# Weight-sum stores recut and moved to ScalarE's DMA queue, with the first group's token loads in halves

## The chip, the cores and the metric

The kernel runs on one core of a Trainium2 chip. Its metric is device time in microseconds. Before the change the median of three runs is 1089.1 us (1088.97 to 1090.56). The profiles are of one execution each.

TensorE (PE) multiplies, VectorE (DVE) and GpSimd (POOL) do elementwise work, ScalarE (ACT) does activations and copies. A DMA is issued by an engine's instruction queue, here by SyncE (SP, which does nothing else) or by ScalarE, and then runs beside the engines. An issue stands in its engine's program order: what comes behind it waits until it has been issued.

## The reference

Linear attention with exponential features over 8 batches and 8 heads (576 tokens of 64 elements), then a feed-forward layer over all 4608 tokens of 512 elements:

```python
proj = q_or_k @ w_phi                      # 64 -> 128
proj -= max(abs(proj), axis=-1)
phi  = concat(exp(proj), exp(-proj))       # 256 features
kv, z = phi(k).T @ v, sum(phi(k))
x    = (phi(q) @ kv) / (phi(q) @ z + 1e-6) # heads side by side: 4608 x 512
h    = x @ w_in                            # 512 -> 2048
out  = (h - tanh(h)) @ w_out               # 2048 -> 512
```

The two feed-forward weights arrive as 64-bit floats and are decoded on the chip.

## The kernel before

The program is written in the order in which each engine executes it; no planner moves anything. It has two stages.

**Attention.** 32 units (a batch and a pair of heads each) go through a software pipeline. After a ramp for units 0 to 2 the loop runs `period(i)` for i = 3 to 31, then `drain()`. In period i, unit a = i is projected, c = i-1 gets its key-value product, p = i-2 its numerator, r = i-3 its denominator, q = i-4 has its reciprocal denominators spread over partitions, and o = i-5 is finished. The steps that matter here, by engine queue and in order:

- SyncE: `x_store(o)` (L495, xs<-d, 288 KB), `den_recip_load(r)` (L474, dn), `den_spread(q)` (L489, rb<-rr, two transfers of 144 KB), `load_v(a)` (L306, v, 320 KB), `den_store(r)` (L484, rr<-rn), and then at the end of the period `x0_load` (L529, in periods 17 to 20) and the stores of `aside_at(i, 2)` (`ring_store`, L112, wd<-wr).
- ScalarE: copies for the weights (`aside_at(i, False)`), the DMA of a piece of weight (L266 or L271, rawi or rawo, 512 KB), the DMA of unit i+2's q and k (L302, qk, 576 KB, which waits until the projection has read the buffer's old contents), then `denom_copy` (L469, dd), `ksum_copy` (L419, kst), the decoder's first step (L278), exponentials, `kv_copy`, `num_copy(p)` (L465, d<-po) and the last exponential.
- GpSimd: `den_mul(o)` (L492, d<-d,rb, which needs rb), `kadd(c)`, and the sums of weights.
- TensorE: project pj, pa, pt (L326), denominators and key sums (pu, L455 and L413), transposes, `kv` (L392), `num` (L441). The projection pa writes the PSUM bank that `num_copy` of the period before reads, and `num_copy` writes one of three buffers d, which `x_store` must have read: in period i it is the buffer that `x_store(i-5)` empties.

**Weight sums.** The feed-forward layer multiplies 2 x 2 blocks with seven products instead of eight. For that, sums and differences of weight blocks are formed once, split into a high and a low part (`Prep`, tiles wr, in three parts for each of eight blocks k: 512, 512 and 768 KB) and stored to DRAM (wd). Seven of the eight blocks are made during the attention periods, in steps that hang on a table `aside`: entry i holds what period i adds on ScalarE, on GpSimd and, third, as stores. Block n (in order) begins at period o = 5, 8, 12, 15, 19, 22, 26.

**Tokens.** The feed-forward layer takes its tokens from xs in groups of 768. Those of group 0 are loaded while attention still runs, as four blocks of 384 KB, each two chunks of 128 features by 384 tokens (`x0_load`). The sums that use them run in periods 30 and 31 and in the drain.

**Feed-forward.** `head()`, `frame(q)` and `finish()`: 48 steps, all after the attention stage. They load the stored weight sums again (L976).

Of the kernel before, what the change touches and what calls it, by code (L numbers as in the profile page):

```python
# [28 lines left out]
def f32(ap):  # L29
    return ap.bitcast(F32)  # L30
# [3 lines left out]
def tile_linear_attention_moe(  # L34
# [10 lines left out]
    nc = tc.nc  # L45
# [14 lines left out]
    HT = TG // 2  # L60
# [27 lines left out]
    xs = [dram.tile([NHP, P, PC], F32, name=f"xs{i}") for i in range(NBP)]  # L88
# [3 lines left out]
    wi, wo, ring, xop = {}, {}, {}, {}  # L92
    xop_pool, st_pool, xst = {s: xo for s in XO_FIRST}, [stp], {}
# [14 lines left out]
    def flat(t):  # L108
        return f32(t).rearrange("p a n f -> p (a n f)")

    def ring_store(q, n, a=0, b=None, queue=nc.sync):
        queue.dma_start(wd[q % NFP][n][:, a:b], flat(ring[q][n])[:, a:b])  # L112
# [96 lines left out]
    def st_any(n, shape, nm):  # L209
        pool = st_pool[n == 2]  # L210
        return pool.tile(shape, F32, tag=f"st{n}", name=nm)

    def st_tile(g, n, nm):
        xst[g, nm] = st_any(n, [P, 2, HT], f"xst{g}{nm}")
        return xst[g, nm]
# [11 lines left out]
    with ExitStack() as c1:  # L227
# [71 lines left out]
        def load(u, queue=nc.sync):  # L299
            u.qk = pq.tile([P, PC], F32, tag="qk", name=f"qk{u.i}")  # L300
            for o, w in ((0, PC),) if u.i else ((5 * P, PC), (0, 5 * P)):
                queue.dma_start(u.qk[:, o:w], qkT[u.i][:, o:w])  # L302
# [6 lines left out]
        def project(u, parts):  # L309
            for part in parts:  # L310
                if u.t is None:
                    u.t = [pq.tile([P, 2, 5, F], F32, tag="t0", name=f"t{u.i}_0"), None]
                    u.m = [p2.tile([P, 2, 5], F32, tag="m0", name=f"m{u.i}_0"), p2.tile([P, 2, 4], F32, tag="m1", name=f"m{u.i}_1")]
                if part == "j":
                    u.pj = ps_pj.tile([P, 2, 512], F32, tag="pj", name=f"pj{u.i}")
                    bank, tiles = u.pj, range(4)
                elif part == "t":
                    u.pt = ps_t.tile([P, 2, 512], F32, tag="pt", name=f"pt{u.i}")
                    bank, tiles = u.pt, range(4, 5)
                else:  # L320
                    u.pa = ps_d.tile([P, 2, 512], F32, tag="po", name=f"pa{u.i}")
                    bank, tiles = u.pa, range(5, 9)
                for k, a in enumerate(tiles):
                    for e in range(2):
                        hs = slice(e * D, (e + 1) * D)
                        nc.tensor.matmul(  # L326
                            bank[:, e, k * F : (k + 1) * F], u.qk[hs, a * P : (a + 1) * P], wph[hs, :], start=True, stop=True
                        )
# [10 lines left out]
        def centre(u, parts, h=None):  # L339
            for part in parts:  # L340
                x, m, t = part_of(u, part)
                if h is not None:
                    x, m, t = x[:, :, h], m[:, :, h], t[:, :, h]
                nc.vector.tensor_reduce(m, x, AX.X, ALU.max, apply_absolute_value=True)
                nc.vector.tensor_tensor(t, x, m.unsqueeze(3).broadcast_to(list(t.shape)), ALU.subtract)  # L345
# [54 lines left out]
        def kadd(u):  # L400
            x = p2.tile([P, 2, 2, F], F32, tag="ss", name=f"ss{u.i}")
            nc.gpsimd.tensor_tensor(x, u.kp[:, :, 1], u.kp[:, :, 2], ALU.add)
            nc.gpsimd.tensor_tensor(x, x, u.kp[:, :, 3], ALU.add)
            nc.gpsimd.tensor_tensor(x, x, u.kp[:, :, 4], ALU.add)
            nc.gpsimd.tensor_tensor(x, x, u.kp[:, :, 0], ALU.add)
            u.ss = x
# [60 lines left out]
        def denom_copy(u):  # L467
            u.dd = pd.tile([P, CH], F32, tag="dd", name=f"dd{u.i}")
            nc.scalar.activation(u.dd, u.pd, AF.Identity, bias=bias_t[:, 3:4])  # L469
# [21 lines left out]
        def den_mul(u, pin=lambda ins: ins):  # L491
            pin(nc.gpsimd.tensor_tensor(u.d, u.d, u.rb, ALU.mult))  # L492

        def x_store(u):
            nc.sync.dma_start(xs[u.b // 2][u.hp, :, (u.b % 2) * S : (u.b % 2 + 1) * S], u.d)  # L495
# [17 lines left out]
        def unit(i):  # L513
            return units[i] if 0 <= i < NU else None

        def bank():
            return ps_c.tile([P, 512], F32, tag="pu", name="pu")
# [5 lines left out]
                    nc.tensor.transpose(u.pq[e][:, j * P : (j + 1) * P], u.t[0][:, e, j, :], ident)  # L523
            q_turn_rest(u, u.pt[:, 0])

        def x0_load(n):
            m, c, h = ((0, 0, 0), (4, 0, 1), (6, 1, 1), (1, 1, 0))[n]
            dst = st_tile(0, 1, "b12") if m == 4 else f32(xop[0][m][:, 1])
            nc.sync.dma_start(dst, xs[0][2 * c : 2 * c + 2, :, h * HT : (h + 1) * HT].rearrange("c p t -> p c t"))  # L529

        def x0_sum(n, eng=nc.gpsimd):
            x = xop[0]
            b11, b21, b22 = (f32(x[m][:, 1]) for m in (0, 1, 6))
            b12 = xst[0, "b12"]
            if n == 0:
                eng.tensor_tensor(st_tile(0, 3, "t1"), b12, b11, ALU.subtract)
            if n == 1:
                eng.tensor_tensor(b12, b22, b12, ALU.subtract)
            if n == 2:
                eng.tensor_tensor(st_tile(0, 4, "t2"), b22, xst[0, "t1"], ALU.subtract)  # L540
            if n == 3:
                eng.tensor_tensor(st_tile(0, 0, "b21"), b21, xst[0, "t2"], ALU.subtract)
# [12 lines left out]
        aside = collections.defaultdict(lambda: ([], [], []))  # L555
        for n, k in enumerate(order[:EARLY_K]):
            p = Prep(k, nc.gpsimd, early_tile, early_stage).steps()
            o = 5 + 7 * (n // 2) + 3 * (n % 2)
            acts = ((1, "h2"), (2, "h4 h6"), (3, "h0")) if n % 2 == 0 else ((2, "h2 h6"), (3, "h4 h0"))
            work = (  # L560
                ((0, "s1 s3 s2"), (1, "s4 l2"), (2, "l4 l6"), (3, "l0"))
                if n % 2 == 0
                else ((0, "s1"), (1, "s3 s2 s4"), (2, "l2 l6"), (3, "l4 l0"))
            )
            for which, x in enumerate((acts, work)):
                for d, names in x:
                    aside[o + d][which].extend(p[nm] for nm in names.split())
            if True:
                when = (3, 4, 5, 5) if n % 2 else (2, 3, 4, 5)
                for d, (part, a, b) in zip(when, ((1, 0, 1024), (2, 0, 768), (2, 768, 1536), (0, 0, 1024))):  # L570
                    aside[o + d][2].append(lambda k=k, part=part, a=a, b=b: ring_store(k, part, a, b))
        aside[30][1].extend(lambda n=n: x0_sum(n) for n in range(2))
        aside[31][1].append(lambda: x0_sum(2))

        def aside_at(i, late):
            for f in aside[i][late]:
                f()
# [57 lines left out]
        def period(i):  # L635
            a, c, p, r, q, o = (unit(i - n) for n in range(6))
            w = dec[i - 3]
            if i < NU - 1:
                aside_at(i, False)
            if o:  # L640
                den_mul(o)
                x_store(o)
            project(a, "jat")
            centre(a, "jt")
            kadd(c)
            aside_at(i, True)
            dec.append(dec_load(i - 2, nc.scalar))
            if i + 2 < NU:
                load(units[i + 2], nc.scalar)
            pu = bank()  # L650
            if r:
                denom(r, pu)
            ksum(p, pu)
            if r:
                denom_copy(r)
                den_recip_load(r)
            if q:
                den_spread(q)
            if i > 3:
                load_v(a)  # L660
            ksum_copy(p)
            kv_turn(p)
            kv_turn_copy(p)
            dec_0(w, a.pt)
            q_turn(c)
            ksum_turn(p)
            q_turn_rest(c, pu)
            q_exp(c)
            q_exp_rest(c)
            ksum_turn_copy(p)  # L670
            centre(a, "a")
            k_exp(a, 0)
            kv(c)
            kv_copy(c)
            k_exp(a, 1, (0,))
            dec_1(w)
            dec_2(w)
            if r:
                den_recip(r)
                den_store(r)  # L680
            dec_3(w)
            if i == NU - 1:
                x0_split(0)
            if 17 <= i < 21:
                x0_load(i - 17)
            aside_at(i, 2)
            num(p)
            num_copy(p)
            if i < NU - 1:
                k_exp(a, 1, (1,))  # L690
# [610 lines left out]
```

## Time and profile before

| | |
|---|---|
| median of the runs | 1089.1 us (1088.97 to 1090.56) |
| profiled execution, its own time | 1092.86 us |
| its span | 1090.8 us |
| granted TensorE clock, mean | 0.997 |
| attention periods 3 to 31 begin | 23.68 us to 299.66 us |

Instructions are named by line, engine, operation and tile: "L326 PE MATMUL pj<-wph,qk" writes pj from wph and qk. An engine's name with a q (ACTq, SPq) is its instruction queue, where DMA issues stand; their duration is that of the issue, not of the transfer. In the chain of waits "DMA xs<-d" is a transfer from its issue to its landing. "[1.88 <-PE pu L413]" is the engine's idle time just before, and what ended it. In a table of windows each row is a stretch of the span: its length, then busy time of each engine with the count of instructions, then the granted clock of TensorE as a share of full speed, the mean busy share of the 16 DMA engines and what they moved in GB/s.

### The profile page before, as it was taken

The page shows a single profiled execution, that of the slowest core. Times are in us where ns is not written, and L with a number is a line of the kernel's source. Part 1 is how long each engine was busy: PE and PEld are TensorE (multiplying, and loading weights), DVE is VectorE, ACT ScalarE, POOL GpSimd, SP SyncE. Part 2 cuts the span into 40 slices and gives each one's busy share as a digit, 9 for nine tenths or more (in the row PEclk, how much of TensorE's full clock was granted, in tenths as well). Part 3 has the DMA queues.
Part 4 walks back from the last instruction along what each step waited for, and adds up shares of the span by engine and source line. Part 5 has one row for each costly group of instructions (what it writes and reads, how often), then busy time and mean ns, then how long its engine had stood idle before and what let it go on. Part 6 is the DMA issues. An engine that isn't in the chain of part 4 may idle for free.

```text
span 1090.8 us, 19205 instructions
## 1 busy us (share of the span) xinstructions
PE 1066.3 (98%) x7244; PEld 891.1 (82%) x7244; DVE 958.8 (88%) x1207; ACT 861.6 (79%) x1349; POOL 273.5 (25%) x236
## 2 busy tenths in 40 slices
PE   8999999899999999999999999999999999999998
PEld 6666666567657888889899889989899989989997
DVE  7999898799888999988998889988998889988877
ACT  5888887688788878887788878887778878887775
POOL 4788987789890000000000000000000000000000
PEclk9999999999999999999999999999999999999999
DMA  5689888979855363355434533355333543453311
GB/s 179 183 244 271 267 267 255 294 215 282 263 171 165 109 224 131 116 176 196 131 107 160 202 116 107 124 186 174 107 124 127 180 158 117 134 173 108 117 49 58
DMA packets 75100, 184.59 MB, mean 169 GB/s; under 512 B 15616, under 2 KB 30336, under 8 KB 75008
## 3 DMA queue, kind: packets, MB, share of 16 engines
q1 hardware_dynamic: 60608, 150.99, 42.6%
q10 hardware_dynamic: 14400, 32.38, 9.4%
q8 instruction: 57, 0.93, 0.4%
q14 instruction: 35, 0.29, 0.1%
HBM read 149.49 MB, written 33.70 MB: 168 GB/s over the span
## 4 chain that ended last, share of the span: by engine, by line
PE 78%; DVE 7%; DMA 7%; ACT 3%; issue 2%; POOL 1%; SPq 1%; ACTq 0%; DVEq 0%; POOLq 0%
PE A L142 16%; PE B L142 12%; PE po L936 11%; PE po L935 11%; PE po L941 10%; DMA xs<-d 4%; PE pc L392 4%; PE po L441 3%; PE pu L455 3%; PE pa L326 2%; DMA rb<-rr 2%; PE pj L326 2%; PE ptt L356 2%; POOL d L492 1%; DVE s2y L895 1%
## 5 line engine op out<-in xcount | busy, mean ns | idle before, releaser
L142 PE MATMUL A<-xo,wr 128*128 128x384 f32 x1152 | 233.8, 338 | 2.3 <-ACT u L855 2.2
L142 PEld LDWEIGHTS A<-xo,wr 128*128 128x128 f32 x1152 | 205.3, 188 | 16.3 <-ACT u L855 3.4
L142 PE MATMUL B<-xo,wr 128*128 128x384 f32 x864 | 176.9, 340 | 4.5 <-DVE hx L862 2.5
L142 PEld LDWEIGHTS B<-xo,wr 128*128 128x128 f32 x864 | 153.7, 189 | 11.9 <-DVE hx L862 6.0
L855 ACT COPY u<-A 128x384 f32<-128x384 f32 x144 | 69.0, 480 | 92.6 <-PE A L142 92.1
L935 PE MATMUL po<-who,ghy 128*128 128x512 f32 x288 | 113.0, 392 | 1.1 <-ACT ghy L910 1.1
L935 PE MATMUL po<-who,ghx 128*128 128x512 f32 x288 | 113.4, 394 | 0.2 <-DVE hy L866 0.2
L936 PE MATMUL po<-wlo,ghx 128*128 128x512 f32 x288 | 113.2, 393 | 0.0
L936 PE MATMUL po<-wlo,ghy 128*128 128x512 f32 x288 | 112.9, 392 | 0.0
L492 POOL TENSOR_TENSOR d<-d,rb 128x576 f32<-128x576 f32 x32 | 45.5, 1423 | 217.9 <-DMA rb<-rr 206.9
L381 ACT ACTIVATE kp<-t 64x256 f32<-64x256 f32 (+1 forms) x126 | 88.5, 727 | 2.1 <-DVE t L345 1.0
L941 PE MATMUL po<-who,glx 128*128 128x512 f32 x288 | 81.5, 391 | 0.0
L941 PE MATMUL po<-who,gly 128*128 128x512 f32 x282 | 79.8, 391 | 0.0
L392 PE MATMUL pc<-kp,v 128*64 128x256 f32 x640 | 76.1, 384 | 0.5 <-DVE kv L434 0.5
L910 ACT CAST ghy<-s2y 128x768 fp32r<-128x768 f32 x47 | 39.3, 837 | 43.9 <-DVE s2y L904 43.9
L892 DVE SCALAR_TENSOR_TENSOR s1x<-s1x,yx 128x768 f32<-128x768 f32 (+1 forms) x49 | 46.2, 942 | 27.6 <-ACT s1x L880 27.2
L441 PE MATMUL po<-qe,kv 128*64 128x288 f32 x512 | 68.0, 408 | 0.0
L941 PEld LDWEIGHTS po<-who,glx 128*128 128x128 f32 x288 | 54.0, 188 | 12.0
L392 PEld LDWEIGHTS pc<-kp,v 128*64 128x64 f32 x640 | 43.0, 136 | 24.4 <-issue 4.5
L941 PEld LDWEIGHTS po<-who,gly 128*128 128x128 f32 x282 | 52.9, 188 | 11.8
L935 PEld LDWEIGHTS po<-who,ghy 128*128 128x128 f32 x288 | 54.0, 188 | 9.7 <-ACT ghy L910 1.4
L935 PEld LDWEIGHTS po<-who,ghx 128*128 128x128 f32 x288 | 54.3, 189 | 9.1 <-DVE hy L866 0.7
(179 smaller groups left out, 2441.4 us busy)
## 6 DMA issues: line engine op xcount, KB each, us to landing
wr<-wd SPq DMA_DIRECT2D x92, 512.0 KB
wr<-wd SPq DMA_DIRECT2D x46, 768.0 KB
qk<-in_qkT ACTq DMA_DIRECT2D x27, 576.0 KB
v<-in_v SPq DMA_DIRECT2D x32, 320.0 KB
rb<-rr SPq DMA_DIRECT2D x64, 144.0 KB
xs<-d SPq DMA_DIRECT2D x32, 288.0 KB
out<-o SPq DMA_DIRECT2D x35, 256.0 KB
rawo<-in_moe_w_out ACTq DMA_DIRECT2D x16, 512.0 KB
```

The lines of the kernel that those rows point to most:

```text
L142: nc.tensor.matmul(bank[:, 0:HT], w[:, a, n, cs], x[:, b, c, :], start=start and i == 0, stop=i == 5, skip_group_check=not start,)
L326: nc.tensor.matmul(bank[:, e, k * F : (k + 1) * F], u.qk[hs, a * P : (a + 1) * P], wph[hs, :], start=True, stop=True)
L381: nc.scalar.activation(u.kp[h, :, j, s, :], u.t[r][h, :, x, :], AF.Exp, scale=1.0 - 2.0 * s)
L392: nc.tensor.matmul(u.pc[e * D : (e + 1) * D, 0 : 2 * F], u.v[:, j, e, :], u.kp[:, e, j, :, :], start=(j == first), stop=(j == last))
L441: nc.tensor.matmul(u.po[e * D : (e + 1) * D, c, 0:CH], u.kv[:, s, e * D : (e + 1) * D], u.qe[:, e, s, c * CH : (c + 1) * CH], start=(s == ...
L492: pin(nc.gpsimd.tensor_tensor(u.d, u.d, u.rb, ALU.mult))
L855: nc.scalar.copy(t, A[q][:, 0:HT])
L892: nc.vector.scalar_tensor_tensor(z.s1[:, s], z.s1[:, s], PC1, z.y[:, s], ALU.add, ALU.mult)
L910: nc.scalar.copy(z.gh[:, s], z.s2[:, s])
L935: nc.tensor.matmul(po, z.gh[:, ts], wh, start=first, stop=False)
L936: nc.tensor.matmul(po, z.gh[:, ts], wl, start=False, stop=False)
L941: nc.tensor.matmul(po, z.gl[:, ts], wh, start=False, stop=last)
```

## The change

The stores of a block's sums are cut anew, so that each of the periods 8 to 31 stores 512 KB (period 7: 256 KB). Before it was 384, 512 or 896 KB. There are 35 stores instead of 28. Each of the four token loads becomes two of 192 KB, one for each chunk, in consecutive periods: periods 9 and 10, 11 and 12, 16 and 17, 18 and 19, instead of 17 to 20. Both kinds are issued by ScalarE instead of SyncE. Their place in the period moves: from its end to just behind the DMA of unit i+2's q and k, ahead of the denominators. In periods 8 to 22 and 27 to 29 ScalarE issues two of them, in the others of 7 to 31 one.

```diff
-        def x0_load(n):
+        def x0_load(n, j):
             m, c, h = ((0, 0, 0), (4, 0, 1), (6, 1, 1), (1, 1, 0))[n]
-            dst = st_tile(0, 1, "b12") if m == 4 else f32(xop[0][m][:, 1])
-            nc.sync.dma_start(dst, xs[0][2 * c : 2 * c + 2, :, h * HT : (h + 1) * HT].rearrange("c p t -> p c t"))
+            if m == 4 and j == 0:
+                st_tile(0, 1, "b12")
+            dst = xst[0, "b12"] if m == 4 else f32(xop[0][m][:, 1])
+            nc.scalar.dma_start(dst[:, j], xs[0][2 * c + j, :, h * HT : (h + 1) * HT])
...
-            if True:
-                when = (3, 4, 5, 5) if n % 2 else (2, 3, 4, 5)
-                for d, (part, a, b) in zip(when, ((1, 0, 1024), (2, 0, 768), (2, 768, 1536), (0, 0, 1024))):
-                    aside[o + d][2].append(lambda k=k, part=part, a=a, b=b: ring_store(k, part, a, b))
+            pieces = (
+                ((2, 1, 0, 512), (3, 1, 512, 1024), (3, 2, 0, 512), (4, 2, 512, 1536), (5, 0, 0, 1024))
+                if n % 2 == 0
+                else ((3, 1, 0, 1024), (4, 2, 0, 1024), (5, 2, 1024, 1536), (5, 0, 0, 512), (6, 0, 512, 1024))
+            )
+            for d, part, a, b in pieces:
+                aside[o + d][2].append(lambda k=k, part=part, a=a, b=b: ring_store(k, part, a, b, nc.scalar))
+        for i, m in ((9, 0), (11, 3), (16, 1), (18, 2)):
+            for c in range(2):
+                aside[i + c][2].append(lambda m=m, c=c: x0_load(m, c))
...
             if i + 2 < NU:
                 load(units[i + 2], nc.scalar)
+            aside_at(i, 2)
             pu = bank()
...
-            if 17 <= i < 21:
-                x0_load(i - 17)
-            aside_at(i, 2)
             num(p)
```

## The prediction

> **What bounds the kernel now.** I read the page first: busy shares and the chain that ended last.
>
> ```profile
> span 1090.8 us, 19205 instructions
> PE 1066.3 (98%) x7244; PEld 891.1 (82%) x7244; DVE 958.8 (88%) x1207; ACT 861.6 (79%) x1349; POOL 273.5 (25%) x236
> PE 78%; DVE 7%; DMA 7%; ACT 3%; issue 2%; POOL 1%; SPq 1%; ACTq 0%; DVEq 0%; POOLq 0%
> qk<-in_qkT ACTq DMA_DIRECT2D x27, 576.0 KB
> v<-in_v SPq DMA_DIRECT2D x32, 320.0 KB
> rb<-rr SPq DMA_DIRECT2D x64, 144.0 KB
> xs<-d SPq DMA_DIRECT2D x32, 288.0 KB
> rawo<-in_moe_w_out ACTq DMA_DIRECT2D x16, 512.0 KB
> ```
>
> TensorE is the bound, yet 7% of the chain is DMA. Only the attention periods move in this change. The timeline of TensorE gives their starts (the pj projections of L326): period 3 at 23.68, period 8 at 71.46, period 31 at 299.66. A table of windows, each from one such start to the next, shows periods 9, 13, 14, 18 to 22, 27 and 29.
>
> ```profile
> 23.68 1.06 PE L326 MATMUL pj<-wph,qk 64*128 64x128 f32 x16
> 71.46 1.16 PE L326 MATMUL pj<-wph,qk 64*128 64x128 f32 x16
> 299.66 1.16 PE L326 MATMUL pj<-wph,qk 64*128 64x128 f32 x16
> core 0: us, PE busy (x) PEld busy (x) DVE busy (x) ACT busy (x) POOL busy (x), PEclk, DMA share, GB/s
> 80.88:90.30 9.42, 9.42 (x111) 6.54 (x109) 8.61 (x14) 7.29 (x15) 8.42 (x8) 1.00 0.88 245
> 118.57:128.57 10.00, 9.75 (x111) 6.64 (x109) 8.71 (x14) 8.15 (x16) 8.79 (x8) 1.00 0.88 263
> 128.57:138.00 9.43, 9.43 (x112) 6.55 (x110) 8.55 (x12) 7.96 (x17) 8.79 (x8) 1.00 0.89 284
> 166.26:175.69 9.43, 9.43 (x111) 6.56 (x110) 8.55 (x12) 8.33 (x17) 9.06 (x8) 1.00 0.81 251
> 175.69:186.87 11.18, 9.82 (x111) 6.63 (x109) 8.57 (x12) 7.39 (x15) 8.00 (x8) 1.00 0.82 255
> 186.87:197.44 10.57, 9.64 (x112) 6.64 (x110) 8.57 (x12) 7.91 (x16) 8.49 (x9) 1.00 0.88 272
> 197.44:209.07 11.63, 9.62 (x112) 6.74 (x110) 8.77 (x12) 8.34 (x17) 9.03 (x8) 1.00 0.96 301
> 209.07:222.70 13.63, 11.21 (x111) 7.68 (x109) 9.07 (x14) 7.88 (x16) 9.31 (x9) 0.87 0.73 231
> 260.40:270.10 9.70, 9.63 (x112) 6.75 (x110) 8.58 (x12) 8.04 (x16) 8.76 (x9) 1.00 0.87 261
> 279.52:290.24 10.72, 9.73 (x112) 6.65 (x110) 8.73 (x14) 8.13 (x16) 8.52 (x8) 1.00 0.93 273
> ```
>
> A clean period is 9.42 us with TensorE busy throughout. 28 periods took 299.66 - 23.68 = 275.98 us; 28 x 9.42 = 263.76; so **12.2 us are stall**, and that is all this change can win. Periods 19 to 22 hold 1.76 + 1.15 + 2.21 + 4.21 = 9.3 of it, 1.8 of these being slow clock (busy 11.21 against 9.42, granted clock 0.87) after the longest stall. They follow the periods 17 to 20 that load the group's tokens. The waits in the attention stage and a stretch of the chain name the loop:
>
> ```profile
> POOL d L492 <- DMA rb<-rr: 19.1, 10, 2.9
> ACT d L465 <- DMA xs<-d: 9.4, 7, 2.7
> PE pa L326 <- ACT d L465: 8.3, 7, 2.4
> 171.86 7.23 DMA rb<-rr
> 179.23 1.42 POOL d L492
> 180.66 7.51 DMA xs<-d
> 188.27 0.65 ACT d L465
> ```
>
> The spread denominators (rb) land late, GpSimd's den_mul starts late, the store of its result (xs) is issued late and lands late, num_copy waits for that buffer, and the next projection waits for num_copy's PSUM bank. From rb's issue to num_copy there are 188.27 - 171.86 = 16.4 us, of which 14.7 are two transfers.
>
> **The change, part by part.**
>
> *The transfers.* A period moves 288 + 512 + 576 + 288 + 320 = 1984 KB (2.03 MB) without stores or token loads. Stores now add 384 to 896 KB, and in periods 17 to 20 token loads add 384 KB more: there the extra is on average 384 + (512 + 512 + 384 + 896) / 4 = 960 KB, in all 3.01 MB. The highest rate in the table is 301 GB/s at a share of 0.96: 3.01 MB need 10.0 us, more than a period has, so the queue grows through four periods. Afterwards stores are 512 KB in each of the periods 8 to 31: 2.56 MB, 8.5 us. Eight periods (9 to 12, 16 to 19) carry 192 KB of tokens besides: 2.75 MB, 9.1 us of 9.42. That fits, but with 0.3 us to spare, while the loop has two transfers that wait in that queue. What those eight periods lose is not in this trace. Lower bound 0: period 14 began with 896 KB of stores just issued and took 9.43. Upper bound: the four heavy periods' mean loss without the clock's share, (9.3 - 1.8) / 4 = 1.9 us, scaled by the extra (704 KB against 960, over the 512 that fit), 0.8 us each. I take 0.4, midway, as the rate leaves no room for bursts: 3.2 us for eight (0 to 6.4).
>
> *The remaining stalls.* The rest of the 12.2 is 2.9 us. Period 29 lost 1.30 after period 27's and 28's stores; single losses in periods 13 (0.58) and 27 (0.27) came in periods with 512 or 384 KB. Another 71.46 - 23.68 - 5 x 9.42 = 0.7 lies in periods 3 to 7, ahead of the first store, and stays. Even stores remove the 1.30 and leave the kind of the others: some 0.06 us in each of 17 ordinary periods, 1.0 us (0 to 2.2).
>
> *Where a store stands in line.* It leaves the end of SyncE's period, ahead of the next xs, and goes behind qk on ScalarE's queue, ahead of rb and v. The sum of what rb and xs wait for is unchanged if transfers are served in the order of issue, whichever queue. Period 6 speaks for that: SyncE's queue had only a 4.5 KB store ahead of xs, yet xs took 7.64 us behind a qk that ScalarE had issued 0.14 us earlier.
>
> ```profile
> 54.43 0.34 ACTq L302 DMA_DIRECT2D qk<-in_qkT  x1
> 54.57 0.32 SPq L495 DMA_DIRECT2D xs<-d  x1
> 54.57 7.64 DMA xs<-d
> ```
>
> The Trainium skill, page "DMA: Bandwidth & Descriptors", section "Queues, rings and completion order", says otherwise: each DMA engine takes turns between the rows it has work for, a packet from each. By it the stores would no longer hold up xs and rb at all; that is a rival below.
>
> *ScalarE.* Stores and loads move from SyncE, which has room, to ScalarE: 35 stores (28 before) and 8 loads (4 before). They stand behind the qk load and ahead of denom_copy (dd) and ksum_copy. The timeline of period 9, and over the stage the issue times (minimum/median/maximum):
>
> ```profile
> 81.10 0.62 ACT L465 COPY d<-po 128x576 f32<-128x576 f32 x1
> 81.87 1.06 PE L326 MATMUL pa<-wph,qk 64*128 64x128 f32 x16
> 83.20 0.33 ACTq L302 DMA_DIRECT2D qk<-in_qkT  x1
> 84.55 0.50 ACT L469 ACTIVATE dd<-pu,bias_t 128x288 f32<-128x288 f32 x1 [1.88 <-PE pu L413]
> 85.40 0.65 ACT L278 ACTIVATE pt<-rawi 128x512 f32<-128x512 f32 x1 [0.19 <-DVE t L345]
> L112 SPq DMA_DIRECT2D wd<-wr x28: 397/432/1330, 71.7 to 309.8; - x28
> L302 ACTq DMA_DIRECT2D qk<-in_qkT x27: 334/334/1247, 25.9 to 283.1; - x27
> ```
>
> qk's issue ends at 83.53, dd begins at 84.55: a hole of 1.02 us, in which ScalarE waits for TensorE anyway. One issue of 0.43 fits; two, 0.86 and two gaps of some 0.05, just fit. Periods 8 to 22 and 27 to 29 have two, none has three. Beyond the hole ScalarE has 0.19 us of idle before the decode step, and num_copy ends at 81.72 where pa starts at 81.87: a cushion of about 0.3 us, after which lateness is TensorE's. A median issue therefore costs nothing. A long one (up to 1.33, 0.9 over the median) in a full hole costs up to 0.6 us. Some 43 issues with, as an estimate, one in ten long, some of these in a half-empty hole: 1.5 us (0 if none collides; if every pair overran as the longest does, 18 x 0.6 = 11 us more). SyncE's own line gets shorter: rr, xs and rb never follow a store's issue; xs is gated by den_mul and gains nothing from that.
>
> *Waits that the issues carry.* A store needs the splits of the period before or earlier, the loads need xs stores three or more periods old: both done. The program also hands its DMAs eight completion semaphores in turn, and an issue waits until the DMA eight back has landed (below, v waits for a token load it has nothing to do with).
>
> ```profile
> SPq L306 <- DMA xst0b<-xs: 1.1, 1, 1.1
> ```
>
> With ten DMAs in a period the weight load on ScalarE waits for the first store of the period before, and qk for the second. These are served ahead of that period's rb, which in a period without stall has landed when den_mul starts, and qk is not issued until 2.3 us into the period (83.20 - 80.88): hidden. If transfers run later by more than about 1 us, ScalarE blocks there, and behind it stand the stores, dd, the denominators' copies and num_copy, for which TensorE waits.
>
> **The sum** on the profiled execution: stall after 3.2 + 1.0 + 0.7 + 1.5 = 6.4 us instead of 12.2, a gain of 5.8; the clock's 1.8 us goes with the long stall. The profiled execution took 1092.86 us (its span is 2.06 shorter), 3.8 above the median of 1089.1. If that excess is stall, the runs shown have 8.4 to lose, and the gain is in proportion 4.0. I take 5: **1084 us**. Bounds of the unknowns: all small ones at nothing leave 0.7 of stall, 11.5 off, 1077.6; the eight periods at 6.4 and the ordinary ones at 2.2, with 0.7 and 1.5, leave 10.8 of 12.2, 1.4 off, 1087.7.
>
> **Rivals.**
>
> *All stalls but the start's go* (0.14): xs, 288 KB, has less ahead of it because stores are issued after it, or because queues take turns. For it: where den_mul starts by 0.7 us into the period, xs goes out ahead of qk. Against: period 6 above, and den_mul is often later (179.23 in a period begun at 175.69). It gives 1089.1 - 11.5 = 1077.6.
>
> *No gain* (0.25): the eight token periods saturate and stall at 0.8 each or a little more, since 2.75 MB at the 272 GB/s of period 20 would be 10.1 us. Stall is then spread, not removed: 1087 to 1091, say 1088.5. For it: the bytes are the same as before. Against: the 301 GB/s of period 21, and period 14.
>
> *Slower* (0.13): ScalarE's hole is too small. If a store's issue right behind qk takes more than 0.65 us instead of 0.43, or if qk waits for a semaphore, two issues pass the hole and the cushion (1.02 + 0.3 = 1.3), and the rest falls on TensorE every period. At 0.95 us each it is 0.6 x 18 = 10.8 us; with the 5 won elsewhere, 1089.1 + 5.8 = 1095. For it: the cushion is thin, and num_copy already ends when pa starts. Against: only a minority of issues are long by the row above (median 0.432, close to the minimum).
>
> My forecast has the remaining 0.48.
>
> **Chances and range.** About 0.2% (2.2 us) is what a measurement of this kernel can tell from no change. Forecast and first rival are faster, but for some 0.02 of the forecast: 0.60. The second rival, mostly within 2.2 us, with that 0.02: 0.26. The third and a little of the second: 0.14. The range reaches from the first rival's time to past no change, leaving out most of the third: 1077.5 to 1091.5. The likeliest case by itself spans 1080 to 1087.
>
> **What would show it.** In the profile after: L112 and L529 on ACTq behind qk; dd still 3.67 us after each period's pj (84.55 - 80.88); windows of periods 19 to 22 near 9.5 to 10 us, at clock 1.00; the wait of num_copy for xs down from 9.4 us to some 4; periods 9 to 12 now the worse ones, with a DMA share of 0.95 or more. Wrong would be: dd late in every two-issue period (third rival), or stalls of a microsecond in periods 9 to 12 and 16 to 19 (second).

## The result, and the profile after

The change is slower: 1104.4 us (1102.6 to 1106.6) against 1089.8 (1089.0 to 1092.5), a ratio of 1.013 with a 95% interval of 1.010 to 1.016. The forecast was 1084.0 in a range of 1077.5 to 1091.5, so it was wrong in its sign. The profiled execution of the changed kernel took 1103.25 us, its span 1101.2. From the page of the kernel after, the chain that ended last, by engine and by line:

```profile
PE 71%; DMA 11%; DVE 7%; ACT 4%; issue 2%; POOL 2%; ACTq 1%; SPq 1%; DVEq 0%; POOLq 0%
PE A L142 16%; PE B L142 12%; PE po L942 11%; PE po L941 11%; PE po L947 10%; DMA xs<-d 4%; DMA rb<-rr 4%; PE pc L392 3%; DMA dn<-dd 2%; PE po L441 2%; PE pa L326 2%; PE pu L455 1%; POOL d L492 1%; PE pj L326 1%; PE ptt L356 1%
```

The share of DMA in the chain rose from 7% to 11%: rb from 2% to 4%, and dn, which the page before does not name, has 2%. All of the loss lies in the attention periods. The windows of the kernel before, periods 3 to 31 and then the rest:

```profile
23.68:299.66 275.98, 267.64 (x3056) 185.43 (x3052) 242.29 (x339) 219.46 (x423) 231.86 (x196) 0.99 0.84 255
309.08:1090.80 781.72, 768.88 (x3878) 684.16 (x3876) 691.34 (x839) 621.36 (x886) 20.22 (x14) 1.00 0.41 139
```

The windows of the kernel after: periods 9 to 12, then 19 to 22, then periods 3 to 31, and the rest:

```profile
81.23:91.24 10.01, 9.77 (x112) 6.63 (x110) 8.58 (x12) 7.17 (x15) 6.82 (x7) 1.00 0.84 259
91.24:101.80 10.56, 9.62 (x112) 6.74 (x110) 8.65 (x12) 8.34 (x17) 9.95 (x10) 1.00 0.85 270
101.80:112.12 10.32, 10.00 (x112) 6.79 (x110) 8.56 (x12) 8.18 (x17) 8.33 (x8) 1.00 0.81 248
112.12:124.22 12.10, 10.03 (x111) 6.70 (x109) 8.57 (x12) 7.28 (x15) 9.79 (x10) 1.00 0.83 253
...
186.41:197.73 11.32, 9.85 (x112) 6.73 (x110) 8.56 (x12) 7.15 (x15) 10.30 (x10) 1.00 0.84 263
197.73:208.54 10.81, 9.78 (x111) 6.64 (x109) 8.57 (x12) 7.68 (x16) 8.24 (x7) 1.00 0.81 243
208.54:219.18 10.64, 9.80 (x111) 6.71 (x109) 8.56 (x12) 8.07 (x17) 8.64 (x8) 1.00 0.80 235
219.18:229.30 10.12, 9.82 (x112) 6.71 (x110) 8.56 (x12) 7.88 (x16) 7.90 (x7) 1.00 0.86 252
...
24.02:310.45 286.43, 270.41 (x3057) 186.16 (x3053) 241.28 (x339) 219.22 (x423) 231.98 (x196) 1.00 0.80 246
319.87:1101.20 781.33, 768.85 (x3878) 684.20 (x3876) 690.82 (x839) 620.80 (x886) 20.00 (x14) 1.00 0.42 138
```

The engines do the same work as before. Against the clean 263.76 us of the 28 periods, the stall grew from 12.2 to 286.43 - 263.76 = 22.7 us. The rest of the kernel is where it was. The shape changed too: before, a few periods lost much; now nearly every period from 9 on loses 0.5 to 2.7 us. And the DMA engines are *less* busy: 0.80 of the stage instead of 0.84, 246 GB/s instead of 255. So the periods don't lack bandwidth in the mean. Something arrives late.

The waits of the attention stage name candidates. The kernel after (waited in all in us, times, longest):

```profile
POOL d L492 <- DMA rb<-rr: 37.4, 24, 3.0
DVE rn L479 <- DMA dn<-dd: 31.2, 20, 2.5
ACT d L465 <- DMA xs<-d: 11.5, 11, 1.7
PE pa L326 <- ACT d L465: 10.6, 13, 1.5
PE pu L422 <- ACT kst L419: 3.6, 5, 0.9
PE ptt L356 <- DVE t L345: 1.7, 7, 0.3
```

The last three rows are TensorE's own waits: together all of its idle time in periods 3 to 31 (286.43 - 270.41 = 16.0 us; the rest of the stall shows as longer busy time). Before, the idle time was 275.98 - 267.64 = 8.3 us, all of it waiting for num_copy.

VectorE's wait for dn in the kernel before:

```profile
DVE rn L479 <- DMA dn<-dd: 10.5, 8, 2.4
```

VectorE's reciprocal (L479) waits for dn, a transfer of 4.5 KB, three times as long as before. A stretch of the chain of waits after (start, length, what):

```profile
159.88 7.07 DMA dn<-dd
166.98 0.21 DVE rn L479
167.22 3.31 DMA rr<-rn
...
170.64 6.67 DMA dn<-dd
```

And VectorE's timeline after, at the start of period 13 (124.22):

```profile
125.35 0.22 DVE L479 RECIPROCAL rn<-dn 128x9 f32<-128x9 f32 x1 [2.28 <-DMA dn<-dd]
125.48 0.63 DVE L290 SCALAR_TENSOR_TENSOR wi<-rawi,pt 128x512 uint32<-128x512 uint32 x1
126.03 1.22 DVE L344 TENSOR_REDUCE m<-pj 128x8 f32<-128x1024 f32 x1
```

dn, 4.5 KB, is on its way for 6.7 and 7.1 us here. By the completions in the traces, its median over periods 8 to 30 is 6.1 us after and 5.0 before, and its issue starts 5.4 us into a period instead of 4.2; it lands 11.4 us after the period's start instead of 9.5. Its reader takes 0.2 us, but it stands in VectorE's line ahead of the decode step and of the row maxima (L344) of the next projection, and VectorE has little to give: by the windows it is busy 8.6 us of a clean period's 9.42. A wait of 2.28 us therefore makes all that follows some 1.5 us late, as an estimate from these two figures. The late reciprocal also sends rr late, and with it rb, den_mul and xs: the loop that the prediction described, entered at an earlier station.

### The profile page after: what moved, and what is told of

The parts are those of the page before. It is cut to its first block, busy times and chain, and to the rows that moved or that the text cites. A ratio compares the mean times of both kernels' runs of the same rounds, so it can differ in the third digit from the quotient of the medians.

```text
span 1101.2 us, 19215 instructions
## 1 busy us (share of the span) xinstructions
PE 1069.4 (97%) x7244; PEld 892.2 (81%) x7244; DVE 957.3 (87%) x1207; ACT 860.6 (78%) x1349; POOL 273.5 (25%) x236
## 3 DMA queue, kind: packets, MB, share of 16 engines
q10 hardware_dynamic: 20592, 46.80, 14.1%
## 4 chain that ended last, share of the span: by engine, by line
PE 71%; DMA 11%; DVE 7%; ACT 4%; issue 2%; POOL 2%; ACTq 1%; SPq 1%; DVEq 0%; POOLq 0%
PE A L142 16%; PE B L142 12%; PE po L942 11%; PE po L941 11%; PE po L947 10%; DMA xs<-d 4%; DMA rb<-rr 4%; PE pc L392 3%; DMA dn<-dd 2%; PE po L441 2%; PE pa L326 2%; PE pu L455 1%; POOL d L492 1%; PE pj L326 1%; PE ptt L356 1%
## 5 line engine op out<-in xcount | busy, mean ns | idle before, releaser
L898 DVE SCALAR_TENSOR_TENSOR s1x<-s1x,yx 128x768 f32<-128x768 f32 (+1 forms) x49 | 46.1, 942 | 27.7 <-ACT s1x L886 27.3
```

Of the source, the lines that this page charges most:

```text
L898: nc.vector.scalar_tensor_tensor(z.s1[:, s], z.s1[:, s], PC1, z.y[:, s], ALU.add, ALU.mult)
```

## The experiments

Ratios are against the kernel before, timed in between on the same chip (medians 1091.5 to 1092.0; 1089.8 for the change itself). "Place" is where the stores and token loads are issued in a period; "stall" is the length of periods 3 to 31 in the profiled execution, less 263.76; that execution can lie up to 3 us off the median.

| run | cut | issued by | place | median us | ratio (95%) | stall | VectorE waits for dn |
|---|---|---|---|---|---|---|---|
| before | old | SyncE | end of period | 1089.8 | 1 | 12.2 | 10.5 |
| the change | new | ScalarE | behind qk | 1104.4 | 1.013 (1.010 to 1.016) | 22.7 | 31.2 |
| a_recut_only | new | SyncE | end of period | 1088.7 | 0.997 (0.995 to 0.999) | 7.1 | 8.0 |
| b_sync_new_place | new | SyncE | behind xs, ahead of dn | 1099.4 | 1.007 (1.005 to 1.010) | 19.6 | 34.3 |
| b2_behind_dn | new | SyncE | behind dn, ahead of rb, v | 1084.7 | 0.992 (0.989 to 0.995) | 4.3 | 4.3 |
| d_behind_v | new | SyncE | behind v | 1084.4 | 0.995 (0.992 to 0.998) | 2.7 | 3.8 |
| i_old_cut_behind_dn | old | SyncE | behind dn, ahead of rb, v | 1086.0 | 0.995 (0.993 to 0.997) | 3.5 | 3.1 |
| f_move_alone | old | ScalarE (loads: SyncE, end) | behind qk | 1103.2 | 1.009 (1.006 to 1.012) | 21.4 | 15.5 |
| h_stores_only | new | ScalarE (loads: SyncE, end) | behind qk | 1102.0 | 1.010 (1.007 to 1.013) | 20.7 | 27.9 |
| g_scalar_behind_dn | new | ScalarE | after the decode step's first activation | 1099.2 | 1.007 (1.004 to 1.009) | 17.0 | 20.4 |
| e_scalar_behind_v | new | ScalarE | after ksum_turn_copy | 1095.0 | 1.003 (1.000 to 1.005) | 15.6 | 1.6 |

**The new cut alone.** a_recut_only takes the new sizes and the halved loads, and leaves issuer and place as they were.

```diff
-            nc.scalar.dma_start(dst[:, j], xs[0][2 * c + j, :, h * HT : (h + 1) * HT])
+            nc.sync.dma_start(dst[:, j], xs[0][2 * c + j, :, h * HT : (h + 1) * HT])
...
-                aside[o + d][2].append(lambda k=k, part=part, a=a, b=b: ring_store(k, part, a, b, nc.scalar))
+                aside[o + d][2].append(lambda k=k, part=part, a=a, b=b: ring_store(k, part, a, b, nc.sync))
...
                 load(units[i + 2], nc.scalar)
-            aside_at(i, 2)
             pu = bank()
...
                 x0_split(0)
+            aside_at(i, 2)
             num(p)
```

> The new cut and the halved token loads in their new periods, but issued by SyncE at the end of the period as before the change. Three theories of the loss are on the table. Line: the stores now stand in front of dn, rb and v in the order in which transfers are served, so dn reaches VectorE late. Semaphores: with ten DMAs in a period the load of v must wait until xs has landed, because they share one of eight completion semaphores in turn; v and rr behind it on SyncE are late. ScalarE: its issues delay denom_copy. None of the three is at work here, so by all of them the loss of 14.6 us is gone; what is left is the effect of even stores, for which I forecast 1080 to 1087 us. If evening the stores is worth nothing, 1088 to 1091.

It is 0.3% faster, 2.9 us by the medians, and the stall fell by 5.2 us. So the even cut does what it says; the loss comes with the move.

**The new place, issued by SyncE.** b_sync_new_place keeps the change's text but for the engine: on SyncE the same place stands behind xs and ahead of dn.

```diff
-            nc.scalar.dma_start(dst[:, j], xs[0][2 * c + j, :, h * HT : (h + 1) * HT])
+            nc.sync.dma_start(dst[:, j], xs[0][2 * c + j, :, h * HT : (h + 1) * HT])
...
-                aside[o + d][2].append(lambda k=k, part=part, a=a, b=b: ring_store(k, part, a, b, nc.scalar))
+                aside[o + d][2].append(lambda k=k, part=part, a=a, b=b: ring_store(k, part, a, b, nc.sync))
```

> The change with the stores and token loads issued by SyncE instead of ScalarE, at the new place in the period (on SyncE behind xs, ahead of dn) and with the same semaphores. Line and semaphores: still slow, 1098 to 1107 us. ScalarE: the loss is gone, 1084 to 1091.

1099.4, a ratio of 1.007 where the change has 1.013: about half of the loss is there although ScalarE issues none of these transfers. The waits of this run:

```profile
ACT dd L469 <- PE pu L413: 50.5, 28, 3.5
DVE rn L479 <- DMA dn<-dd: 34.3, 24, 2.7
POOL d L492 <- DMA rb<-rr: 29.9, 20, 2.6
PE ptt L356 <- DVE t L345: 5.0, 17, 0.3
PE pt L326 <- DVE wi L290: 4.1, 5, 1.4
PE pa L326 <- ACT d L465: 0.5, 1, 0.5
```

VectorE waits for dn as long as with the change, but the lateness reaches TensorE by another way: here TensorE waits 11.3 us for VectorE (2.2 of it for a tile wo, beside the two rows shown) and 0.5 us for num_copy, with the change 1.7 and 10.6.

**Only dn's place.** b2_behind_dn differs from it in one line: the issue moves from just ahead of dn's to just behind it. rb and v stay behind the stores in both.

```diff
                 load(units[i + 2], nc.scalar)
-            aside_at(i, 2)
             pu = bank()
...
                 den_recip_load(r)
+            aside_at(i, 2)
             if q:
                 den_spread(q)
```

> Stores and token loads issued by SyncE just behind dn and ahead of rb, where the run before had them just ahead of dn (1099.4 us). Only the place of the 4.5 KB transfer dn in the line changes; v still waits for the semaphore of xs. Theory dn (VectorE waits for dn, which stands behind stores): most of the loss goes, 1084 to 1091 us, and VectorE's wait for dn falls from 33 us to under 10. Theory rb (rb and v behind the stores make den_mul and xs late) and theory semaphores (v waits for xs): 1096 to 1101, no real change.

It is 14.7 us faster than b_sync_new_place by the medians (the intervals of the ratios are far apart), and faster than the kernel before by 0.8%. Its waits:

```profile
POOL d L492 <- DMA rb<-rr: 23.0, 19, 3.1
DVE rn L479 <- DMA dn<-dd: 4.3, 5, 1.2
```

The wait for dn fell by 30 us, the wait for rb by 7, and the stall by 15.3. That singles out dn: 4.5 KB that stood behind up to 704 KB. At the median of periods 8 to 30 dn lands 8.7 us into a period here and 11.4 us in b_sync_new_place. Of the difference 1.1 us is its issue, which stood behind those of the stores, and 1.5 us the transfer (4.1 us against 5.6).

**Behind v.** d_behind_v issues them on SyncE behind v's load as well, and has x_store written behind the qk load. Against b_sync_new_place:

```diff
-                x_store(o)
             project(a, "jat")
...
                 load(units[i + 2], nc.scalar)
-            aside_at(i, 2)
+            if o:
+                x_store(o)
...
                 load_v(a)
+            aside_at(i, 2)
             ksum_copy(p)
```

> New cut and halved token loads, issued by SyncE right behind the load of v (about 6.7 us into a period), so behind dn, rb and v in the line and ahead of rr; v shares no semaphore with xs. Line: as fast as the new cut at the old place, 1080 to 1088 us, perhaps better by a few us, because the stores start 3 us earlier. Semaphores and ScalarE: the same range. Slow, 1095 or more, only if rr behind the stores is what is missed.

1084.4, and the smallest stall of all, 2.7 us; against b2_behind_dn the intervals overlap. Waits on an xs are still in SyncE's queue here (13.3 us ahead of token loads, 11.8 ahead of stores), so such waits alone don't make a kernel slow.

**The place alone, with the old cut.** i_old_cut_behind_dn is the kernel before, with nothing but the issue moved from the end of the period to behind dn.

```diff
                 den_recip_load(r)
+            if 17 <= i < 21:
+                x0_load(i - 17)
+            aside_at(i, 2)
...
-            if 17 <= i < 21:
-                x0_load(i - 17)
-            aside_at(i, 2)
             num(p)
```

> The kernel before (uneven stores, whole token loads in periods 17 to 20, SyncE), with only the place moved from the end of the period to just behind dn's issue. If the place gives most of what the even cut at that place gave (1084.7 us against 1092 before): 1084 to 1087 us. If the even cut gives its part by itself (3 us, as at the old place): 1087 to 1090 us, with the stalls of periods 19 to 22 still there. No gain from the place alone: 1090 to 1093 us.

1086.0, 5.5 us under the kernel before, with the same bytes in the same uneven pieces on the same queue. The windows of its periods 14 and 19 to 22, and of periods 3 to 31:

```profile
128.70:138.12 9.42, 9.42 (x111) 6.56 (x110) 8.73 (x14) 8.12 (x17) 5.99 (x6) 1.00 0.97 333
175.81:185.24 9.43, 9.43 (x112) 6.56 (x110) 8.63 (x14) 7.30 (x15) 8.45 (x8) 1.00 0.98 327
185.24:195.42 10.18, 9.62 (x111) 6.61 (x109) 8.57 (x12) 7.78 (x16) 9.81 (x10) 1.00 0.81 256
195.42:206.64 11.22, 9.69 (x111) 7.22 (x110) 8.66 (x12) 8.53 (x17) 6.68 (x6) 1.00 0.94 315
206.64:216.06 9.42, 9.42 (x111) 6.56 (x109) 8.73 (x14) 7.60 (x15) 9.11 (x9) 1.00 0.86 289
24.26:291.56 267.30, 264.80 (x3057) 184.31 (x3053) 242.07 (x339) 218.46 (x423) 230.95 (x195) 1.00 0.85 264
```

Periods 19 to 22 lose 2.6 us where the kernel before lost 9.3. Periods 14 and 19 run clean at a DMA share of 0.97 and 0.98, with 333 and 327 GB/s, above the 301 that the prediction took for the highest rate. Most of the stall of before was thus a matter of order, not of the sizes that the change evened out.

**The move alone, on ScalarE.** f_move_alone takes the old cut; its stores go to ScalarE behind qk, the token loads stay where they were.

```diff
-                    aside[o + d][2].append(lambda k=k, part=part, a=a, b=b: ring_store(k, part, a, b))
+                    aside[o + d][2].append(lambda k=k, part=part, a=a, b=b: ring_store(k, part, a, b, nc.scalar))
...
                 load(units[i + 2], nc.scalar)
+            aside_at(i, 2)
...
                 x0_load(i - 17)
-            aside_at(i, 2)
             num(p)
```

> The move alone: stores with the old cut (384 to 896 KB in a period) issued by ScalarE behind qk; token loads as before the change, by SyncE at the end of periods 17 to 20. If the place in the line is the cause, slow like the change or worse, 1099 to 1112 us. If the number of DMAs in a period (ten instead of nine, and the semaphores shared thereby) is the cause, clearly faster than the change, 1090 to 1096, since most periods then have nine.

1103.2: the move brings the loss without the new cut. VectorE's wait at L479 is put down partly to dn (15.5 us) and partly to rb here:

```profile
DVE rn L479 <- DMA rb<-rr: 11.0, 8, 2.5
SPq L484 <- DMA xs<-d: 55.0, 20, 5.0
```

The last row is SyncE's: most periods have nine DMAs here, so that rr (L484), and no longer v, is the eighth DMA behind xs and waits for it to land. The run does not separate the new place from these shared semaphores.

**Stores moved, token loads not.** h_stores_only is the change with the halved loads back on SyncE at the end of the period.

```diff
-            nc.scalar.dma_start(dst[:, j], xs[0][2 * c + j, :, h * HT : (h + 1) * HT])
+            nc.sync.dma_start(dst[:, j], xs[0][2 * c + j, :, h * HT : (h + 1) * HT])
...
-                aside[i + c][2].append(lambda m=m, c=c: x0_load(m, c))
+                aside[i + c][3].append(lambda m=m, c=c: x0_load(m, c))
...
                 x0_split(0)
+            aside_at(i, 3)
             num(p)
```

> The change's stores on ScalarE at the new place, but the halved token loads on SyncE at the old place, at the end of a period. dn theory: 24 periods still have dn behind 512 KB of stores, so nearly all of the loss stays: 1098 to 1104 us, VectorE's wait for dn above 20 us. Rival, that the loss comes from the eight periods with two kinds of transfers (704 KB): 1086 to 1091 us, wait for dn under 12 us.

1102.0 with 27.9 us of waiting for dn: the stores alone make nearly all of the loss, and the eight periods with two kinds of transfers are not special.

**On ScalarE, but later.** e_scalar_behind_v and g_scalar_behind_dn keep ScalarE as the issuer and move the issue.

```diff
                 load(units[i + 2], nc.scalar)
-            aside_at(i, 2)
             pu = bank()
...
             ksum_turn_copy(p)
+            aside_at(i, 2)
             centre(a, "a")
```

> The change with its issues kept on ScalarE, but 5 us later in the period: behind the copy of the turned key sums (about 7 us in), so behind dn, rb and v in the line. Theories dn and rb: as fast as SyncE behind v, 1082 to 1090 us. If issuing on ScalarE itself costs (its exponentials follow there without idle time), 1092 or more.

The wait for dn is nearly gone (1.6 us), yet 1095.0, 10.7 us above d_behind_v. A few periods lose much. Its waits, and ScalarE's timeline where period 27 ends:

```profile
ACT kp L381 <- DMA xs<-d: 10.5, 7, 2.7
PE pa L326 <- ACT d L465: 10.1, 7, 2.4
```

```profile
269.96 0.29 ACT L426 COPY ks<-pu 128x128 f32<-128x128 f32 x1
272.54 0.33 ACTq L112 DMA_DIRECT2D wd<-wr  x1
272.92 0.72 ACT L381 ACTIVATE kp<-t 64x256 f32<-64x256 f32 x2 [2.66 <-DMA xs<-d]
```

A store has its turn at 270.25 and is issued at 272.54: it waits for an xs that it doesn't touch. In the program's instructions this store, the second of period 27, waits on the completion semaphore that the same period's xs uses, as it is the eighth DMA behind it.

Behind the blocked issue stand the exponentials (kp) and num_copy, for which TensorE waits. On SyncE the same wait holds up only other issues. For g the place is some 0.8 us earlier (its first issue starts 4.5 us into a period that is not delayed, against 5.3):

```diff
                 load(units[i + 2], nc.scalar)
-            aside_at(i, 2)
             pu = bank()
...
             dec_0(w, a.pt)
+            aside_at(i, 2)
             q_turn(c)
```

> The change's own stores and loads on ScalarE, but issued behind the decode step's first activation, so about 5 us into a period and behind dn's issue; the cut and the completion semaphores are the change's (v still shares one with xs). If dn's place behind the stores is the main cause: VectorE's wait for dn falls from 31.2 us to under 6 us, and the time to 1085 to 1091 us. If the cause is that ScalarE issues them, or that v waits for xs's semaphore: 1097 us or more, with the wait for dn little changed. Between the two if ScalarE's issues at that place delay the exponentials: dn's wait gone and 1091 to 1096, with ScalarE's own waits for an xs as in the run behind ksum_turn_copy (10.5 us).

1099.2, and it does not tell the theories apart as it was meant to. The place is behind dn in the text, but the two engines reach their issues together; period 8 has

```profile
75.39 0.60 SPq L474 DMA_DIRECT2D dn<-dd  x1
75.72 1.08 ACTq L112 DMA_DIRECT2D wd<-wr  x2
```

dn's issue lasts to 75.99, the store's starts at 75.72, so the store is beside dn and not behind it. Over periods 8 to 31 the first store or load starts between 0.8 us ahead of dn's issue and 0.8 us behind it. The wait for dn fell only to 20.4 us, and SyncE's waits for an xs ahead of v's load stayed (46.1 us in 17 waits).

**Two that told less.** c_semaphores was to give v another completion semaphore than xs's, by writing x_store behind ScalarE's issues.

```diff
-                x_store(o)
             project(a, "jat")
...
             aside_at(i, 2)
+            if o:
+                x_store(o)
             pu = bank()
```

> The change with every engine's order as it is, only that the program hands xs its completion semaphore after qk, the stores and token loads have theirs; v then shares its semaphore with the weight load and no longer with xs. Semaphores: the loss is gone or nearly, 1082 to 1092 us, and v is issued 6.1 us into a period. Line and ScalarE: 1100 to 1107, as with the change, since dn, rb and the issues stand where they stood.

The edit left the two on one semaphore (v waits 57.1 us for xs), so it is a second run of the change in effect (1106.4, ratio 1.014, 1.011 to 1.016), and says nothing of the semaphores. nodn_after does without dn: the reciprocal is taken of all 128x288 elements, and rr is stored from there.

```diff
...
-            u.dd = pd.tile([P, CH], F32, tag="dd", name=f"dd{u.i}")
+            u.dd = pd.tile([P, CH], F32, tag="dd", name=f"dd{u.i}", bufs=2)
...
+                pin(nc.vector.reciprocal(u.dd, u.dd))
+                return
...
+                nc.sync.dma_start(
+                    u.rr.rearrange("a (c s) -> (a c) s", c=2), u.dd.rearrange("(n r) c -> n r c", r=32)[:, 0, :]
+                )
+                return
...
-                den_recip_load(r)
```

> The change without the transfer dn: VectorE takes the reciprocal of the denominators where ScalarE has put them (128 x 288, 0.1 to 0.2 us more than 128 x 9) and rr is stored from there. Stores stay on ScalarE ahead of rb and v. By the semaphores' turn rr, no longer v, now waits for xs. Theory dn: 1085 to 1093 us. Theory rb: 1097 or more. Theory semaphores: in between or as slow, since rr now carries the wait.

1110.3 (ratio 1.015, 1.012 to 1.019). The price of the edit was misjudged: the reciprocal takes 1.94 us instead of 0.22, more than the 0.8 us that VectorE has free, so this run has a bound of its own and doesn't test dn.

## Why the prediction was wrong

**The step that failed** is "Where a store stands in line": the sentence "The sum of what rb and xs wait for is unchanged if transfers are served in the order of issue, whichever queue". It asked only for rb and xs. The new place is also ahead of dn, which the prediction nowhere names in line, though the wait of L479 for it already stood in the stage's waits of before (10.5 us, 8 times). From the end of the period to ahead of dn costs 10.7 us (a_recut_only to b_sync_new_place), from ahead of dn to behind it wins 14.7. dn is costly to delay: it is the first of the four transfers of the loop, and its reader stands on VectorE, with 0.8 us free in a period.

The step is wrong for xs as well. The stores were to leave the place ahead of the next xs; but with the change a store or token load of the same period is issued ahead of xs in 18 of the 23 periods 8 to 30, since xs itself is issued late (3.8 us into a period at the median, 3.0 before). The wait of num_copy for xs was to fall from 9.4 us to some 4, and rose to 11.5.

That dn's place is a cause is shown on SyncE, by one moved line. That it carries the loss of the change itself to the same extent is argued: VectorE waits for dn as long in both, but TensorE's own waits differ, and no run frees dn with ScalarE as the issuer without another cost.

**The bandwidth** ("That fits, but with 0.3 us to spare") was the wrong limit to price. Periods 9 to 12 were to have a DMA share of 0.95 or more; they have 0.81 to 0.85 and still lose 0.6 to 2.7 us each, while in i_old_cut_behind_dn periods of 0.97 and 0.98 lose nothing. The sign of the rival "No gain", stalls of a microsecond in periods 9 to 12 and 16 to 19, is there, but not for its reason: periods 20 to 22, with stores alone, lose 0.7 to 1.4 us too, and h_stores_only keeps the loss.

**The even cut**, by itself, was sized well: 5.8 us of stall, 4.0 by the medians, taken as 5; a_recut_only lost 5.2 us of stall and gained 2.9 (its interval, 1 to 5 us). But the stalls of periods 19 to 22 were not due to uneven sizes alone, as "the queue grows through four periods" has it: at a better place the uneven cut loses 2.6 there.

**"Waits that the issues carry ... hidden"** looked at ScalarE's raw and qk alone. With ten DMAs in a period v shares a semaphore with the xs eight DMAs ahead of it, and rr is queued behind v; the queue's own waits after:

```profile
SPq L306 <- DMA xs<-d: 61.4, 18, 4.8
```

This is new (33.8 us in b_sync_new_place, 11.2 in b2_behind_dn, with v on the same semaphore as xs). What it costs isn't settled: it shrinks when dn is early (in b2_behind_dn xs is on its way for 4.3 us at the median, in b_sync_new_place 5.5), and d_behind_v is fast with such waits.

**ScalarE.** The rival "ScalarE's hole is too small" has the sign and a part of the mechanism. The issues of a store after have a median of 0.45 us, far from the 0.65 that it needed, but the longest take 2.0:

```profile
L112 ACTq DMA_DIRECT2D wd<-wr x35: 389/446/2032, 64.6 to 311.5; - x35
...
211.83 1.87 ACTq L112
...
213.75 0.07 ACT dd L469
```

Eight of the 43 issues of stores and token loads take more than 0.8 us. Where such an issue ends late, as in the last two rows, from the chain of waits, dd and behind it the key sums kst are late, and TensorE waits for kst: 3.6 us in all, where the prediction's term for ScalarE was 1.5. What makes an issue long isn't shown. In b_sync_new_place dd waits longer (50.5 us), but for TensorE, and TensorE waits nowhere for kst.

ScalarE as the issuer does have a price: 1.013 against 1.007 at the same place in the text, some 6 us, and 10.7 us between e and d. In e the trace shows how: an issue that waits for a semaphore blocks the exponentials behind it. For the 6 us of the change itself the waits of TensorE give two leads: the 3.6 us for kst, and the 10.6 us instead of 0.5 for num_copy, which waits for xs 11.5 us with the change and 0.9 us in b_sync_new_place, where xs is issued ahead of the stores in every period. How the 6 us divide stays open.

**The rival of queues that take turns**, from the Trainium skill, page "DMA: Bandwidth & Descriptors", section "Queues, rings and completion order", does not hold here as the prediction read it: by it the stores in ScalarE's queue would not hold up transfers in SyncE's; yet with the change L479 waits 31.2 us for dn instead of 10.5. The records of the DMA packets show more. In period 16 of the change ScalarE issues rawo, qk, a store and a token load from 157.48 to 159.31, SyncE xs at 159.16 and dn at 159.88. The two queues from 159.0 to 163.4 us, then from 163.4 to 166.5 (packets, MB, busy share of the 16 engines; q10 is ScalarE's, which moves 32.38 MB in the kernel before and 46.80 after):

```profile
q10 hardware_dynamic: 288, 1.12, 92.4%
q1 hardware_dynamic: 3, 0.00, 0.0%
...
q10 hardware_dynamic: 267, 0.64, 52.7%
q1 hardware_dynamic: 398, 0.54, 51.5%
```

For 4.4 us SyncE's queue moves next to nothing, while ScalarE's moves about what rawo and qk hold (1088 KB); then both move side by side, though xs was issued behind the store and the token load. So neither order of issue, which the prediction assumed, nor turns alone describes it. At the median of periods 8 to 30 the first data of SyncE's queue come 3.8 us after xs's issue, against 1.4 before.

The same section says that a transfer's completion signal lands only after every earlier write of that DMA engine, across its queues. That is not where dn's time goes: in the 17 periods where its packets can be told apart, they begin 4.3 us after its issue at the median, and it lands 0.6 us after the last of them.

## What to carry to other kernels

Before a bulk transfer is moved in a period, list every small transfer issued behind it in any queue, and ask for each how much slack its reader's engine has: 4.5 KB for a VectorE that is busy 8.6 of 9.42 us decided more than 512 KB of evenly cut stores. A mean DMA share of 0.84 with stalls asks first for another order, and only then for other sizes; here moving the issue behind dn gave 5.5 us with nothing recut, and with the even cut 0.8%. Issue bulk transfers from an engine whose queue holds nothing that TensorE waits for, since an issue can wait for the completion of an unrelated earlier DMA.

## What the hardware showed that was not expected

- A transfer of 4.5 KB took 5.0 us at the median before, 6.1 with stores issued ahead of it by another engine, 5.6 with stores ahead of it in its own queue, and 4.1 with them behind it (before, the change, b_sync_new_place, b2_behind_dn).
- SyncE's queue moved next to nothing for 4.4 us with two transfers issued, while ScalarE's moved 1.12 MB (the change, 159.0 to 163.4 us); then both moved at once.
- The stage moved 333 GB/s in a period that lost nothing (i_old_cut_behind_dn, period 14), and 253 in one that lost 2.7 us (the change, period 12): the rate says little about who is late.
- VectorE's reciprocal takes 1.94 us for 128x288 elements and 0.22 for 128x9, against 0.41 for a copy of 128x256 on the same engine (kv<-pc).
